# Four sums of weight quarters from VectorE to GpSimd, and two second-level sums one step later, in routed attention with an MLP

## The chip, the cores and the metric

The kernel runs on one core of a Trainium2 chip. The core has five engines, each with its own instruction stream: TensorE (PE, matmuls), VectorE (DVE), ScalarE (ACT), GpSimd (POOL) and SyncE (SP, which here issues the DMAs). Engines wait for each other by semaphores only. VectorE, ScalarE and GpSimd work on SBUF; GpSimd is not used on PSUM, where the matmul results lie. The metric is the device time of one execution in microseconds, and of several executions the median.

## The reference

Two blocks follow each other. The first is attention with a routing mask: 4 batches, 8 heads, 768 positions, 64 dimensions. Each query and each key is assigned to the nearest of 16 centroids, and a query sees only the keys of its own cluster.

```python
q_assign = argmax(einsum(q_n, c_n)); k_assign = argmax(einsum(k_n, c_n))
scores = where(q_assign == k_assign, q @ k.T / 8, -1e9)
attn = exp(scores - max) / (sum + 1e-9);  out = attn @ v
```

The result, as 3072 tokens of 512 numbers, goes through an MLP with weights w_in (512 x 2048) and w_out (2048 x 512), all in float32:

```python
h = x @ w_in
g = h * erf(softplus(h))
return g @ w_out
```

## The kernel before

**Attention.** Two heads are a pair; there are 16 pairs (0 to 15). Each pair is worked in six periods, i = 0 to 5, written out in `period(p, i)`. A period covers two units, a unit being 128 keys against 384 queries of both heads. For each unit PE forms the masked scores (tile sc), ScalarE takes the exponential (pr), GpSimd adds the pr of a half up (`accumulate`, into part of more_out), and PE multiplies by v (into the PSUM bank turned). At the same time the bounds of the next half are found: PE writes products of lowered q and k to the PSUM tile wide, and VectorE reduces them (nmx). There is one wide tile, so PE cannot write the next pass before nmx has been read. At i = 3, `similarities` and `choose` begin the routing of the pair after the next: PE writes a turned bank, VectorE transposes it to sims, and PE needs that bank again for the sums of `divide`, which form at i = 0 and i = 3 from GpSimd's accumulated sums.

**Weights.** During attention w_in and w_out are also loaded and brought to the form in which the MLP uses them: ScalarE (`size`, `rest`, `sign`), VectorE (`bounded`, `shifted`) and GpSimd (`summed`) work on one block after another; in the profile these are the VectorE and GpSimd steps on w_out in pairs 9 to 15.

**Forms.** The MLP's matrix products use seven block products in place of eight, and for that sums and differences of the quadrants of w_in are made ahead, called forms. `left_forms` gives four of them for a pair of column groups f and f + 1: new[0] = a21 + a22, new[1] = new[0] - a11, a21 = a11 - a21, new[2] = a12 - new[1]. The new ones lie in more_in, the third replaces a part of w_in. The column groups f = 0, 2, 4, 6 give four quarters, 16 forms, each a 128 x 512 step. They stand in the list `forms`, in order, each with a version for VectorE and one for GpSimd; four forms of x for chunk 0 are appended behind pair 13. `FORMS` says how many VectorE takes in which period of which pair, and `POOL_FORMS` in which pairs GpSimd takes one at i = 1. What is left at the end, VectorE takes. Before, GpSimd takes 8 of the w_in forms in pairs 8 to 15 and VectorE 8, of which four lie in pairs 12, 13 and 14.

**Behind the attention.** The MLP works in chunks of 512 tokens. `hidden(0, 0)` makes the first half of the hidden columns of chunk 0 (quarters 0 and 1), `hidden(0, 1)` the second half (quarters 2 and 3). Each has four rounds of seven products, and VectorE and ScalarE add the products up from PSUM banks: six that rotate, and two, turned, from the end of attention on. Beside this, the last four blocks of w_out are made ready (`weights`, in `aside_work`), and GpSimd makes second-level forms: `forms_twice` builds 18 sums from w_in and its forms, in the staging tiles a_s and x_own, and each is stored to DRAM (w_dram) by an SP issue. Their order is fixed: four are made at once behind the attention, three ahead of GpSimd's first `summed`, eight behind a fence in `hidden(0, 1)`, and the rest (three) behind that stage. The staging tile x_own is the place of x of chunk 1, so `load_x(1)` waits for the last store. The fences are one-column steps of GpSimd that wait for a step of VectorE.

**Order.** TensorE, VectorE, ScalarE and GpSimd instructions stay in the order in which the program records them, and so do the SP issues of the attention; the SP issues behind it are placed by the scheduler and then run in that order. Line L137 in the profile is the helper through which nearly all of these instructions are recorded, so groups are told apart by tile names.

Of the kernel before, what the change touches and what calls it, by code (L numbers as in the profile page):

```python
# [35 lines left out]
HT, HK, HF, HM = CT // 2, DM // P // 2, NFT // 2, DM // 2  # L36
# [1 line left out]
LC = 512  # L38

UP = 2.0**16  # L40
FORMS = {12: {0: 1}, 13: {0: 1}, 14: {0: 1, 3: 1}, 15: {0: 1, 3: 2, 4: 2, 5: 2}}
POOL_FORMS = range(8, 16)
BIG = 2.0**60
FLOOR = 2.0**50
EPS = 2.0**-70
# [71 lines left out]
BY_VECTOR = 4  # L117
MADE_BEFORE = (3, 0, 0, 0)
MADE = (0, 8)
LAST_AT = (3, 6, 9, 12, 15, 18, 21)  # L120
EARLY_OUTERS = 6
STORE_AFTER = 2
# [23 lines left out]
def kernel(  # L146
# [13 lines left out]
    te, ve, ae, ge = (  # L160
        InOrder(tc, e, in_order) for e in (nc.tensor, nc.vector, nc.scalar, nc.gpsimd)
    )
# [49 lines left out]
    def part_of(i, lo, n):  # L212
        return more_out[:, i].rearrange("p f m -> p (f m)")[:, lo : lo + n]
# [103 lines left out]
    def size_and_rest(n):  # L317
        size(n)
        rest(n)
# [112 lines left out]
    def vectors(p, nm):  # L432
        if p < NPAIR:
            ae.copy(out=pairs[p][nm + "v"], in_=pairs[p][nm + "T"])
# [139 lines left out]
    def divide(u):  # L574

        p, half, _ = units[u]
        st = pairs[p]
        av = st["av", half]

        psum = turned[1 - half][:, 0:QW]  # L580
        for g in range(4):
            te.matmul(psum[g * Q : (g + 1) * Q], lhsT=minus, rhs=st["acc", half][:, g], start=True, stop=True)

        if u + 1 < len(units):
            inv = routep.tile([P, QW], F32, name="inv")
            den = routep.tile([P, QW], F32, name="den")
        else:
            inv, den = part_of(0, 4 * HW, QW), part_of(1, 0, QW)
        ae.activation(out=inv, in_=psum, func=ACT.Ln, bias=alleps, scale=-1.0)
        ae.activation(out=inv, in_=inv, func=ACT.Exp, scale=-1.0)  # L590
        yield
        ve.scalar_tensor_tensor(
            out=den, in0=psum, scalar=S * EPS, in1=inv, op0=ALU.subtract, op1=ALU.mult
        )
        for k in range(2):
            raw = av[:, k, 0:QW]
            ve.scalar_tensor_tensor(
                out=raw, in0=raw, scalar=av[:, k, QW : QW + 1], in1=inv, op0=ALU.add, op1=ALU.mult
            )
        yield  # L600
        x = part_of(0, (2 * p + half) % 4 * HW, HW).rearrange("p (k x) -> p k x", k=2)
        ve.scalar_tensor_tensor(
            out=x, in0=den.unsqueeze(1).to_broadcast([P, 2, QW]), scalar=2.0, in1=av[:, :, 0:QW],
            op0=ALU.add, op1=ALU.mult,
        )
        b, r = divmod(p, HP)
        for g in range(4):
            rows_of, at = r * P + g // 2 * D, b * S + half * HW + g % 2 * QW
            nc.sync.dma_start(
                out=x_dram[rows_of : rows_of + D, at : at + QW].rearrange("(k r) x -> r k x", k=2),  # L610
                in_=x[g * Q : (g + 1) * Q],
            )
        if half == 1:
            del pairs[p]
        yield
# [16 lines left out]
    def left_forms(engine, a11, a12, a21, a22, new):  # L632

        return [
            functools.partial(plus_of, new[0], a21, a22, engine),
            functools.partial(minus_of, new[1], new[0], a11, engine),
            functools.partial(minus_of, a21, a11, a21, engine),
            functools.partial(minus_of, new[2], a12, new[1], engine),
        ]
# [10 lines left out]
    def lefts(a11, a12, a21, a22, new):  # L650
        return {1: a11, 2: a12, 3: new[2], 4: a22, 5: new[0], 6: new[1], 7: a21}
# [7 lines left out]
    def w_in_parts(f, n):  # L659
        c1, c2 = slice(f * P, (f + n) * P), slice((HF + f) * P, (HF + f + n) * P)  # L660
        return (
            w_in[:, 0:HK, c1], w_in[:, HK:, c1], w_in[:, 0:HK, c2], w_in[:, HK:, c2],
            [more_in[:, i, :, c1] for i in range(3)],
        )
# [317 lines left out]
    def last_forms_twice():  # L982
        work = {}
        for o, p in zip(GROUPS[1][1], LAST_AT):
            w = lefts(*w_in_parts(0, HF))[o]
# [339 lines left out]
    def run(work):  # L1325
        for _ in work:
            pass
# [3 lines left out]
    def step_ahead(u, behind=False):  # L1331
        p, i = divmod(u + NJ, 2 * NJ)
        steps = maxima_step(p, i, behind=behind) if p < NPAIR else iter(())
        if not behind:
            run(steps)
        return steps

    forms = []
    for f in range(0, HF, 2):
        forms += zip(*(left_forms(e, *w_in_parts(f, 2)) for e in (ve, ge)))  # L1340
    routing = [iter(())]
    part = [iter(())]
# [1 line left out]
    def period(p, i):  # L1344
        u = 2 * NJ * p + 2 * i
        n1, n2 = 2 * p - 1, 2 * p
        early = lambda n: 0 <= n < N_EARLY

        def mask(place):
            which = (MASKS if p else FIRST_MASKS).get((i, place))  # L1350
            if which:
                return masks(p + 1, *which, turned[0 if i in (0, 5) else 1], place > 1, ve if i == 0 else ae)
            return lambda: None

        if u > 0:
            for which in turns if i in (0, 3) else ():
                turn(*which)
                turns.remove(which)
            step_ahead(u)
        mask(0)()  # L1360
        next(part[0], None)
        if i == 5:
            next(routing[0], None)
        if i == 0 and p:
            run(routing[0])
        if u == 2:
            next(routing[0])
        products(u)
        products(u + 1)
        mask(1)()  # L1370
        second = step_ahead(u + 1, True) if u > 0 else iter(())
        next(second, None)
        rows = D if u == 0 or u + NJ >= len(units) else Q
        scores(u, rows)
        next(second, None)
        if i:
            next(second, None)
        next(part[0], None)
        scores(u + 1, rows)
        later = mask(2)  # L1380
        if i == 0:
            later()
            later = lambda: None
            next(second, None)
        if i == 3:
            similarities(p + 2)
            routing[0] = choose(p + 2, sc_of[u + 1][:, 0], True)
        curve(u)
        later()
        curve(u + 1)  # L1390
        if u == 0:
            step_ahead(1)
            similarities(1)
            routing[0] = choose(1, turned[0])
            next(routing[0])
            next(routing[0])
            vectors(1, "q")
            vectors(1, "k")
        if i == 0 and early(n1 - 1):
            bounded(n1 - 1)  # L1400
            shifted(n1 - 1)
            sign(n1 - 1)
        elif i == 1 and early(n1):
            size_and_rest(n1)
        elif i == 3 and early(n1):
            bounded(n1)
            sign(n1)
        elif i == 5 and early(n2):
            rest(n2)
        for _ in range(min(len(forms), FORMS.get(p, {}).get(i, 0))):  # L1410
            forms.pop(0)[0]()
        if i == 3:
            next(routing[0], None)
            if early(n1):
                shifted(n1)
            for _ in range(2):
                next(routing[0], None)
        elif i == 1:
            load(p + 1, "v", v, vp)
            if p == 0:  # L1420
                run(routing[0])
                transposes(2, "q")
        elif i == 2:
            transposes(p + 2, "k")
        elif i == 4:
            vectors(p + 2, "k")
            vectors(p + 2, "q")
        elif i == 5:
            transposes(p + 3, "q")
        if u > 0:  # L1430
            if i == 1 and p in POOL_FORMS and forms:
                forms.pop(0)[1]()
            if i == 1 and early(n1 - 1):
                summed(n1 - 1)
            elif i == 4 and early(n1):
                summed(n1)
            for w in (u - 2, u - 1):
                accumulate(w)
            for w in (u - 2, u - 1):
                attend(w)  # L1440
            if i % HJ == 0:
                part[0] = divide(u - 1)
                next(part[0])
        if i == 3 and early(n2):
            size(n2)
# [73 lines left out]
    for w in (u - 2, u - 1):  # L1519
        attend(w)  # L1520
    last = divide(u - 1)
    attention.close()

    psb = pool("psb", 6, space=PSUM)
# [22 lines left out]
        GROUPS[1][1][:EARLY_OUTERS],  # L1547
        (actp.tile([P, 2 * FG * HT], F32, name="a_s"), x_of[1].rearrange("p k t -> p (k t)")),
    )
    for _ in range(4):  # L1550
        next(making)()
    queues[0] = store_queue[0] = nc.sync

# [24 lines left out]
    def make():  # L1578
        next(making, idle(1)[0])()

    aside_work += (
        together(idle(2) + gates(0, 0, (0,)), [make] * MADE[0])
        + [lambda: fence(sums_of[0, 0, 0][:, 2, 0, 0:1])] + [make] * MADE[1]
    )
# [65 lines left out]
```

## Time and profile before

| | us |
|---|---|
| median of three runs | 964.12 (963.8 to 964.22) |
| profiled execution, its own time | 963.84 |
| its span | 962.0 |
| granted TensorE clock | 0.999 |
| pairs 12 to 14 | 314 to about 390 |
| first matmul of the MLP | 411.2 |

The span is that of the engines' instructions; the execution's own time is 1.84 us longer. In a line of a timeline the columns are start, duration, engine, source line, operation, output tile, input tiles, shapes and a count, and in brackets how long the engine stood idle before it and what ended that. A group of equal steps is merged into one line. PE is TensorE with matmuls, PEld its weight loads. The chain of waits follows the work that ended last back through what released it.

### The profile page before, as it was taken

What the parts mean: (1) busy time and instruction counts of PE and PEld (TensorE: products, weight loads), DVE (VectorE), ACT (ScalarE), POOL (GpSimd) and SP (SyncE); (2) the same over time, 40 slices, a digit from 0 to 9 for tenths busy, and PEclk for the clock granted to TensorE, in tenths of its full rate; (3) what the DMA queues carried; (4) which work ended last, traced back from release to release, by engine and by line L of the source; (5) the groups of instructions that cost most, each with busy time, mean ns of one, the idle gap of its engine ahead of it and who ended that gap; (6) DMA issues with size and microseconds to landing.
All of it is one profiled execution on the core that took longest, in us unless ns stands there. A gap on an engine that the chain in (4) does not pass through costs nothing.

```text
span 962.0 us, 22444 instructions
## 1 busy us (share of the span) xinstructions
PE 951.3 (99%) x8954; PEld 727.9 (76%) x8954; DVE 800.8 (83%) x1399; ACT 539.0 (56%) x815; POOL 531.4 (55%) x371
## 2 busy tenths in 40 slices
PE   8999999999999999999999999999999999999998
PEld 3555555555555555588888888998999899989987
DVE  8888888888888887787679889788868987897887
ACT  3777777777777777552523541654257236625541
POOL 1688888888888888877579910360054016202600
PEclk9999999999999999999999999999999999999999
DMA  9345445544554521151403444463445436343533
GB/s 222 63 111 112 111 111 111 112 112 110 105 117 83 116 55 52 27 173 41 168 1 154 171 144 136 136 204 110 154 125 172 113 129 209 110 148 120 154 116 110
DMA packets 172313, 116.06 MB, mean 121 GB/s; under 512 B 131376, under 2 KB 141104, under 8 KB 172208
## 3 DMA queue, kind: packets, MB, share of 16 engines
q1 hardware_dynamic: 169280, 113.41, 42.5%
q8 instruction: 71, 1.16, 0.5%
q10 hardware_dynamic: 2928, 1.21, 0.4%
q14 instruction: 34, 0.28, 0.1%
HBM read 90.21 MB, written 24.38 MB: 119 GB/s over the span
## 4 chain that ended last, share of the span: by engine, by line
PE 95%; DVE 3%; DMA 1%; issue 0%; SPq 0%; ACT 0%; DVEq 0%; ACTq 0%
PE bank L137 42%; PE turned L137 31%; PE sc L137 16%; PE wide L137 6%; DVE nmx L137 1%; DMA out_dram<-osb 0%; DVE w_out L137 0%; DMA in_k<-in_k_dram 0%; DVE osb L137 0%; SPq L137 0%; DVE kT L137 0%; DVE km L137 0%; DVE sims L137 0%; DVE more_in L137 0%; DVE qT L137 0%
## 5 line engine op out<-in xcount | busy, mean ns | idle before, releaser
L137 POOL TENSOR_TENSOR more_out<-more_out,pr 128x768 f32<-128x768 f32 x128 | 217.2, 1697 | 16.9 <-ACT pr L137 7.6
L137 DVE TENSOR_REDUCE nmx<-wide 128x2 f32<-128x768 f32 x189 | 180.5, 955 | 46.4 <-PE wide L137 45.9
L137 ACT ACTIVATE pr<-sc 128x768 f32<-128x768 f32 x192 | 148.7, 810 | 89.8 <-PE wide L137 72.8
L137 POOL TENSOR_TENSOR g<-g 128x512 f32<-128x512 f32 x36 | 47.1, 1309 | 217.6 <-DVE g L137 215.7
L137 PE MATMUL turned<-pr,in_v 128*32 128x193 f32 x3072 | 144.8, 330 | 0.0
L137 PEld LDWEIGHTS turned<-pr,in_v 128*32 128x32 f32 x3072 | 91.5, 109 | 50.7 <-issue 21.3
L137 PE MATMUL sc<-qT,kT 64*128 64x384 f32 x528 | 98.4, 486 | 0.0
L137 DVE TENSOR_TENSOR g<-g 128x512 f32<-128x512 f32 x114 | 79.1, 694 | 16.5 <-PE bank L137 12.9
L137 DVE TENSOR_TENSOR g<-a_s,g 128x512 f32<-128x512 f32 x80 | 72.4, 931 | 5.6 <-ACT a_s L137 5.6
L137 DVE TENSOR_TENSOR g<-bank,g 128x256 f32<-128x256 f32 (+1 forms) x129 | 63.9, 522 | 14.8 <-PE bank L137 7.2
L137 PE MATMUL bank<-w_out,g 128*128 128x256 f32 x328 | 75.7, 380 | 0.0
L137 ACT ACTIVATE a_s<-g 128x1024 f32<-128x1024 f32 (+1 forms) x36 | 41.0, 1149 | 55.9 <-POOL g L137 45.3
L137 PE MATMUL bank<-g_more,g 128*128 128x256 f32 x304 | 71.8, 379 | 0.0
L137 PE MATMUL bank<-x_own,w_in 128*128 128x128 f32 (+1 forms) x432 | 71.6, 308 | 0.0
L137 POOL TENSOR_TENSOR more_out<-pr,pr 128x768 f32<-128x768 f32 x32 | 58.9, 1840 | 19.9 <-ACT pr L137 19.9
L137 PEld LDWEIGHTS bank<-w_out,g 128*128 128x128 f32 x328 | 62.0, 190 | 9.6 <-issue 1.4
L137 PEld LDWEIGHTS <-qv 64*128 64x128 bf16 x384 | 27.0, 93 | 55.2 <-issue 39.2
L137 PE MATMUL wide<-kv,qv 64*128 64x384 bf16 x378 | 64.1, 328 | 2.5 <-DVE nmx L137 1.8
L137 PEld LDWEIGHTS sc<-qT,kT 64*128 64x128 f32 x528 | 49.6, 187 | 21.6 <-ACT inv L137 3.1
L137 ACT ACT_TABLE_LOAD x40 | 51.3, 1283 | 22.8 <-DVE g L137 22.2
L137 PEld LDWEIGHTS bank<-x_own,w_in 128*128 128x128 f32 x432 | 61.1, 191 | 4.0 <-issue 0.6
L137 PEld LDWEIGHTS bank<-g_more,g 128*128 128x128 f32 x304 | 57.8, 190 | 7.9
(243 smaller groups left out, 2062.4 us busy)
## 6 DMA issues: line engine op xcount, KB each, us to landing
g_more<-b_dram SPq DMA_DIRECT2D x48, 512.0 KB, 3.6
g_more<-w_dram SPq DMA_DIRECT2D x84, 256.0 KB, 2.8
x_own<-in_moe_w_in_dram SPq DMA_DIRECT2D x13, 512.0 KB, 5.5
in_v<-in_v_dram SPq DMA_DIRECT2D x32, 192.0 KB, 3.2
x_dram<-more_out SPq DMA_DIRECT2D x128, 48.0 KB, 1.7
x_own<-x_dram SPq DMA_DIRECT2D x6, 1024.0 KB, 5.3
in_k<-in_k_dram SPq DMA_DIRECT2D x59, 96.0 KB, 2.6
in_q<-in_q_dram SPq DMA_DIRECT2D x58, 96.0 KB, 4.9
```

What stands on the lines that cost most here:

```text
L137: ins = getattr(self.engine, name)(*args, **kw)
```

## The change

The list `forms` loses the last quarter: it runs over f = 0, 2, 4 and has 12 forms of w_in. `FORMS` loses its entries for pairs 12, 13 and 14 (four forms) and keeps those of pair 15. GpSimd takes one form in each of pairs 8 to 15 at i = 1, as before (`POOL_FORMS` is now a table of periods). The four forms of the last quarter are made by GpSimd behind the last `accumulate` and ahead of the second-level forms. Of the latter, two (`AHEAD`) in place of four are made at once; all 18 keep their order, so each of the later groups begins two forms earlier in it, and the last group has five in place of three.

```diff
-FORMS = {12: {0: 1}, 13: {0: 1}, 14: {0: 1, 3: 1}, 15: {0: 1, 3: 2, 4: 2, 5: 2}}
-POOL_FORMS = range(8, 16)
+FORMS = {15: {0: 1, 3: 2, 4: 2, 5: 2}}
+POOL_FORMS = {p: (1,) for p in range(8, 16)}
...
+AHEAD = 2
...
     forms = []
-    for f in range(0, HF, 2):
+    for f in range(0, HF - 2, 2):
         forms += zip(*(left_forms(e, *w_in_parts(f, 2)) for e in (ve, ge)))
...
-            if i == 1 and p in POOL_FORMS and forms:
+            if i in POOL_FORMS.get(p, ()) and forms:
                 forms.pop(0)[1]()
...
     last = divide(u - 1)
+    for work in left_forms(ge, *w_in_parts(HF - 2, 2)):
+        work()
     attention.close()
...
-    for _ in range(4):
+    for _ in range(AHEAD):
         next(making)()
```

On the engines this comes to four VectorE instructions fewer and four GpSimd instructions more, two GpSimd instructions with their two SP stores in a later place, and, on PE, a wait for GpSimd at the first three products of the third round of `hidden(0, 1)` that read forms of the last quarter. TensorE's, ScalarE's and SyncE's instructions are the same in kind and number.

## The prediction

> **What bounds the kernel now.** I read the page's table of engines and the chain first, then the waits of PE, then the timelines of PE, VectorE (DVE) and GpSimd (POOL) around each of them. The first two lines say that TensorE is the kernel: 951.3 of 962.0 us, 95% of the chain. Time can be won only where PE stands still.
>
> ```profile
> PE 951.3 (99%) x8954; PEld 727.9 (76%) x8954; DVE 800.8 (83%) x1399; ACT 539.0 (56%) x815; POOL 531.4 (55%) x371
> PE 95%; DVE 3%; DMA 1%; issue 0%; SPq 0%; ACT 0%; DVEq 0%; ACTq 0%
> ```
>
> PE has no wait in the profile between 55 and 306 us, and none after 411 us. Between 306 and 384 us, which are pairs 12 to 14, it has five, 2.61 us in all (0.45 + 0.76 + 0.45 + 0.45 + 0.50):
>
> ```profile
> 318.24 0.34 PE L137 MATMUL wide<-kv,qv 64*128 64x384 bf16 x2 [0.45 <-DVE nmx L137]
> 329.70 0.53 PE L137 MATMUL turned<-more_out,minus 128*32 128x192 f32 x8 [0.76 <-DVE sims L137]
> 344.24 0.34 PE L137 MATMUL wide<-kv,qv 64*128 64x384 bf16 x2 [0.45 <-DVE nmx L137]
> 369.28 0.34 PE L137 MATMUL wide<-kv,qv 64*128 64x384 bf16 x2 [0.45 <-DVE nmx L137]
> 379.84 0.53 PE L137 MATMUL turned<-more_out,minus 128*32 128x192 f32 x8 [0.50 <-POOL more_out L137]
> ```
>
> The km instruction runs once a pair, so its starts are a ruler. Pair 11 lasts 24.47 us, pair 12 26.00, pair 13 25.04; pairs 2 to 7 last 24.43 to 24.45 each by the same row.
>
> ```profile
> 289.97 0.62 DVE L137 TENSOR_SCALAR km<-turned,nbig 128x384 bf16<-128x384 f32 x1 [0.55 <-PE turned L137]
> 314.44 0.62 DVE L137 TENSOR_SCALAR km<-turned,nbig 128x384 bf16<-128x384 f32 x1 [0.55 <-PE turned L137]
> 340.44 0.62 DVE L137 TENSOR_SCALAR km<-turned,nbig 128x384 bf16<-128x384 f32 x1 [0.54 <-PE turned L137]
> 365.48 0.62 DVE L137 TENSOR_SCALAR km<-turned,nbig 128x384 bf16<-128x384 f32 x1 [0.54 <-PE turned L137]
> ```
>
> VectorE's timeline shows what stands in front of the waits. In pair 12 the form (more_in, 0.68 us) lies between two w_out steps and the reduction nmx that PE waits for. Later in the pair a w_out step takes 1.39 us where pair 11's took 0.42, and the transpose sims behind it is late.
>
> ```profile
> 302.64 0.42 DVE L137 TENSOR_SCALAR w_out<-w_out 128x512 f32<-128x512 f32 x1
> ...
> 315.84 0.88 DVE L137 TENSOR_SCALAR w_out<-w_out 128x512 f32<-128x512 f32 x2
> 316.63 0.68 DVE L137 TENSOR_TENSOR more_in<-w_in 128x512 f32<-128x512 f32 x1
> 317.23 0.95 DVE L137 TENSOR_REDUCE nmx<-wide 128x2 f32<-128x768 f32 x1
> 327.68 1.39 DVE L137 TENSOR_SCALAR w_out<-w_out 128x512 f32<-128x512 f32 x1
> ```
>
> GpSimd's timeline gives the reason: in pairs 12 and 14 its own form waits 2.6 us for VectorE's, and its sums of pr then end at 328.8 us, over the slow w_out step; in pair 11 they ended at 302.74.
>
> ```profile
> 295.78 6.96 POOL L137 TENSOR_TENSOR more_out<-more_out,pr 128x768 f32<-128x768 f32 x4
> 317.39 1.27 POOL L137 TENSOR_TENSOR more_in<-more_in,w_in 128x512 f32<-128x512 f32 x1 [2.61 <-DVE more_in L137]
> 321.80 6.98 POOL L137 TENSOR_TENSOR more_out<-more_out,pr 128x768 f32<-128x768 f32 x4
> 368.43 1.27 POOL L137 TENSOR_TENSOR more_in<-more_in,w_in 128x512 f32<-128x512 f32 x1 [2.62 <-DVE more_in L137]
> 427.50 1.30 POOL L137 TENSOR_TENSOR w_out<-w_out,g_more 128x512 int32<-128x512 int32 x1 [1.94 <-ACT w_out L137]
> 450.27 0.19 POOL L137 TENSOR_TENSOR u<-g_more 128x1 f32<-128x1 f32 x1 [5.96 <-DVE g_more L137]
> 487.76 0.19 POOL L137 TENSOR_TENSOR u<-g 128x1 f32<-128x1 f32 x1 [17.90 <-DVE g L137]
> ```
>
> **Part 1: VectorE loses four forms in pairs 12 to 14** (one at i = 0 of each, one at i = 3 of pair 14); 4 x 0.68 us. PE, ScalarE and SyncE keep their instructions. GpSimd still makes one form a pair, but its inputs now come from its own earlier forms, so the two waits of 2.6 us for VectorE have nothing left to wait for. In pair 11, which has the same w_out steps and a GpSimd form but no VectorE form, PE never waits; that is my model for the changed pairs.
> - The waits at i = 0 (three of 0.45): nmx ends 3.18 us behind km in pair 11 (292.20 + 0.95 - 289.97), and PE asked for the bank at 3.35 (318.24 - 0.45 - 314.44). Without the form there is 0.17 us to spare. All three go.
> - The 0.76 in pair 12: without its wait GpSimd's sums end 12.8 us behind km, as in pair 11, and the w_out step starts at 12.7 and takes 0.42 again. It goes. Pair 13, where GpSimd's form had no wait, shows no such stall.
> - The 0.50 in pair 14: GpSimd's sum ended at 379.78, and PE wanted it at 379.34, less 0.45 from the wait before, so 13.4 behind km; at 12.8 the sum is 0.6 us early. It goes.
> The price by pair: 26.00 - 24.47 = 1.53 in pair 12, 25.04 - 24.47 = 0.57 in pair 13 (each a little over its waits, since PE starts again slower), and for pair 14, which has no km behind it, its waits alone, 0.95. Sum -3.05. Ends: -2.61 (waits alone) and -3.3 (pair 14 with the same quarter on top).
>
> **Part 2: pair 15.** VectorE's seven forms and GpSimd's one stand where they stood and are of the same kinds, for other columns. Columns of quarters 0 and 1, which the first hidden block needs at 411 us, are now complete at 391 us (pair 15, i = 0). Cost 0.
>
> **Part 3: GpSimd's four forms behind the last sums.** Each is 1.27 us (the more_in<-more_in,w_in row), 5.1 us, starting at 414.57 in the old clock. ScalarE's first copy of a bank waited 4.65 us for GpSimd; it waits for the last sum of pr, which still stands before the forms, so it is not later. PE needs these columns in the third block row of hidden(0,1), 448 us; they are there at 420. Cover: 28 us. Cost 0.
>
> **Part 4: two second-level forms move back** (2 x 1.27 us and two stores on SP). Until the first weight is summed GpSimd has 5.1 - 2.5 = 2.6 us more: that sum ends at 428.1 instead of 425.56, and the next, due at 427.50, 0.7 us late; the 1.94 us of idle time covers the rest, and the fence with 5.96 us of idle stands behind both. On SP the third and fourth a_s stores come about 1.5 us later, and the four x_dram stores of the last unit queue behind them; these are columns of the last batch, read long after. Behind the fence GpSimd has 13 forms instead of 11: the last three stores become five, the load of x for chunk 1 (issued at 467.7, landed by about 473.5 by the DMA shares) comes 2.6 us later, 476.1. VectorE takes it at 475.99 without waiting now, so it waits about 0.1 us, and the four steps on x end at 478.8 against PE's need at about 485 (chunk 1's first block). The w_out forms behind it end at 472.5 instead of 469.85; the next fence idles 17.9 us. Cost on PE 0; if this cover were gone, at most the 2.6.
>
> **The one doubt is VectorE beside a busier GpSimd** between 425.6 and 428.2, when it empties PE's banks. Its w_out steps there take 0.42 us when GpSimd is idle and 0.84 to 1.49 when it works; steps that read a bank keep 0.41. One or two more become slow: 0.4 to 2.1 us. A bank is refilled after six other fills: the one read at 427.29 to 427.71 is filled again at 429.26, the one done at 427.04 at 428.39, so 1.35 to 1.55 us are to spare. I take 0 (one slow step is 0.4 to 1.07), bounds 0 and 0.8 (two at 1.07 less 1.35).
>
> A rule speaks against the change. The Trainium skill, GPSIMD Engine Reference, section 4.1 Engine selection, gives two-input elementwise work to VectorE, with GpSimd about 2x slower. The rows agree on the ratio (1267 against 683 ns). By the rule the four forms lose 4 x 0.58 = 2.3 us of engine time, and counted on the path the sum would be -0.7 us; by the waits above they leave a place where PE stands and go to one where it does not, and the sum stays -3.05.
>
> **The sum** against the profiled execution's own 963.84 us: 963.84 - 3.05 = 960.8. The median of the runs, 964.12, lies 0.28 above that execution; I say 960.9. A measurement of this kernel can tell about 0.2%, 1.9 us, from no change, so the forecast is faster by more than that (0.32%), with 1.1 us in hand.
>
> **Rivals.**
> - Half of it stays (13%): GpSimd's sums stay late in pairs 12 and 14 for another reason (its w_out sum also waits for ScalarE, 1.1 to 2.4 us in most pairs), so 0.76 + 0.32 of pair 12 and 0.50 stay: 1.58. For it: the slow w_out step meets GpSimd by only 0.1 us in pair 11. Against it: pairs 8 to 11 never stall. Time 963.84 - 1.47 = 962.4.
> - Part is given back in the first hidden stage (8%): two to three slow w_out steps more than the banks cover, 1 to 2 us of PE. Time 961.9 to 962.8.
> - Slower (6%): the same place, but each of the eight w_out steps between 419 and 433 us (1.39, 0.84, 1.49, 0.42, 1.14, 0.42, 0.42, 0.42, together 6.54) takes 1.49: 11.92, so 5.4 us, and the banks cover nothing. It decides from 3.05 us on, and past 5.0 us shows as slower. Time 963.84 - 3.05 + 5.4 = 966.2. Against it: half of these steps run where GpSimd's load is unchanged.
> - The change does nothing (2%): PE waits at the same places for other VectorE work. Time 964.
>
> **Numbers.** Forecast 71%, all faster. The first rival straddles: 3 of its 13 to faster. Second: 3 of 8 to faster. Faster 0.77, same 0.17, slower 0.06. Range: from 963.8 - 3.3 less 0.3 of scatter, 960.2, up to the second rival's 962.8, which takes in the first.
>
> **What would show it.** Right: PE has no wait between 306 and 384 us; km steps of 24.4 to 24.6 us in pairs 12 and 13; GpSimd's forms in pairs 12 and 14 without a wait; the w_out step near 12.7 us behind km at 0.42; four GpSimd forms before the first a_s; PE still without waits from the end of attention on. Wrong: a PE wait on g or on a bank within 25 us of the first bank matmul, a PE wait for x near 74 us behind it, or a sims wait that stays in pair 12.

## The result

| | before | after |
|---|---|---|
| median of seven runs, us | 964.01 (963.73 to 964.22) | 960.8 (960.48 to 961.08) |
| profiled execution, its own time | 963.84 | 960.8 |
| its span | 962.0 | 959.1 |

The ratio is 0.9966, with a 95% interval of 0.9954 to 0.9978: 3.2 us less, where 960.9 us was forecast. On a second chip the same kernel gave 0.9975 (0.9964 to 0.9986), 961.64 against 963.83 us, with single runs from 960.67 to 962.24. A few tenths of a microsecond between two medians therefore say little, and the experiments below are read in their traces: of each stage by its length, and within a stage by the starts of PE's matmuls, which are the same 8954 in the same order in all these kernels and can be compared one by one.

The page of the changed kernel, table of engines and chain: PE has the same work, VectorE four instructions and 3.0 us less, GpSimd four instructions and 6.9 us more, and the span is 2.9 us shorter.

```profile
PE 951.2 (99%) x8954; PEld 727.5 (76%) x8954; DVE 797.8 (83%) x1395; ACT 538.7 (56%) x815; POOL 538.3 (56%) x375
PE 96%; DVE 2%; ACT 1%; issue 0%; DMA 0%; DVEq 0%; SPq 0%; ACTq 0%
```

The trace marks no wait of PE any more behind the first 55 us. It leaves out idle time under 0.15 us and counts it from the end of the matmul ahead; delays that it does not mark are told below. VectorE's timeline has the ruler again (km, once a pair), and behind it in pair 12 the w_out step and the transpose sims:

```profile
314.80 0.62 DVE L138 TENSOR_SCALAR km<-turned,nbig 128x384 bf16<-128x384 f32 x1 [0.55 <-PE turned L138]
339.41 0.62 DVE L138 TENSOR_SCALAR km<-turned,nbig 128x384 bf16<-128x384 f32 x1 [0.55 <-PE turned L138]
363.85 0.62 DVE L138 TENSOR_SCALAR km<-turned,nbig 128x384 bf16<-128x384 f32 x1 [0.55 <-PE turned L138]
...
327.48 0.42 DVE L138 TENSOR_SCALAR w_out<-w_out 128x512 f32<-128x512 f32 x1
327.94 0.58 DVE L138 STREAM_TRANSPOSE sims<-turned 128x384 f32<-128x384 f32 x1
```

GpSimd's timeline of pair 12: the form starts at once, without the wait of 2.61 us, and the four sums end at 327.58, 12.78 us behind km.

```profile
315.08 1.29 POOL L138 TENSOR_TENSOR more_in<-w_in 128x512 f32<-128x512 f32 x1
317.45 1.28 POOL L138 TENSOR_TENSOR w_out<-w_out,x_own 128x512 int32<-128x512 int32 x1 [1.09 <-ACT x_own L138]
320.61 6.97 POOL L138 TENSOR_TENSOR more_out<-more_out,pr 128x768 f32<-128x768 f32 x4
```

Pair 14 has no km behind it, but PE's own sums at i = 0 (turned from more_out and minus) give its length. PE's timeline of the changed kernel:

```profile
364.97 0.51 PE L138 MATMUL turned<-more_out,minus 128*32 128x192 f32 x8
388.73 0.51 PE L138 MATMUL turned<-more_out,minus 128*32 128x192 f32 x8
```

Before, these two started at 366.60 and 391.64. So the kernel by stages, in us:

| stage | before | after | difference |
|---|---|---|---|
| start to km of pair 12 | 314.44 | 314.80 | +0.36 |
| pair 12, km to km | 26.00 | 24.61 | -1.39 |
| pair 13, km to km | 25.04 | 24.44 | -0.60 |
| pair 14, sums at i = 0 to the next | 25.04 | 23.76 | -1.28 |
| pair 15, to the MLP's first matmul | 19.59 | 19.58 | 0 |
| MLP, to the end of the span | 550.77 | 550.79 | 0 |

The gain is 3.27 us, all of it in pairs 12 to 14. The 0.36 at the start were there before any changed instruction (the first km starts at 11.69 us in place of 11.30). Between the km of pair 14 and its sums lie 1.12 us in both kernels, which no row counts. The 0 of the MLP is a sum of two: matmul by matmul, PE falls 0.34 us back at 473 us, which the section on the forms behind the attention explains, and gains 0.38 us at 695 us, at a matmul that before had waited 0.12 us for ScalarE's osb. No changed instruction stands there, and the cause of this gain is open.

### The profile page after: what moved, and what is told of

The parts are those of the page before. It is cut to its first block, busy times and chain, and to the rows that moved or that the text cites. A ratio compares the mean times of both kernels' runs of the same rounds, so it can differ in the third digit from the quotient of the medians.

```text
span 959.1 us, 22447 instructions
## 1 busy us (share of the span) xinstructions
PE 951.2 (99%) x8954; PEld 727.5 (76%) x8954; DVE 797.8 (83%) x1395; ACT 538.7 (56%) x815; POOL 538.3 (56%) x375
## 4 chain that ended last, share of the span: by engine, by line
PE 96%; DVE 2%; ACT 1%; issue 0%; DMA 0%; DVEq 0%; SPq 0%; ACTq 0%
PE bank L138 42%; PE turned L138 32%; PE sc L138 17%; PE wide L138 6%; DVE nmx L138 1%; ACT a_s L138 0%; ACT L138 0%; DVE g L138 0%; DMA in_q<-in_q_dram 0%; DVE kT L138 0%; DVE osb L138 0%; DVE g_more L138 0%; DVE sims L138 0%; DVE qT L138 0%; DVE turned L138 0%
```

## The experiments

What is undecided behind such a table is the cause: the work taken from VectorE, its place in front of nmx, or GpSimd's wait for it; and whether what was put behind the attention is really free. Each kernel below is the changed one with one edit. Both kernels with VectorE's forms, GpSimd busy and four forms ahead ran on a chip on which the changed kernel itself was not run; their medians are read against the kernel before, and their stages against the changed kernel's trace. The traces are compared by the same stages:

| kernel | pair 12 | pair 13 | pair 14 | MLP | median | ratio to before |
|---|---|---|---|---|---|---|
| before | 26.00 | 25.04 | 25.04 | 550.77 | 964.01 | 1 |
| changed | 24.61 | 24.44 | 23.76 | 550.79 | 960.8 | 0.9966 |
| changed, second chip (again) | 24.63 | 24.44 | 23.74 | 550.84 | 961.64 | 0.9975 |
| VectorE's forms, own chain, i = 0 | 25.08 | 25.07 | 24.36 | 550.97 | 962.35 | 0.9984 |
| the same at i = 1 | 24.78 | 24.75 | 24.08 | 550.46 | 961.34 | 0.9976 |
| GpSimd waits (pool_waits) | 25.96 | 24.44 | 25.00 | 550.82 | 963.69 | 0.9999 |
| GpSimd busy (pool_late) | 26.16 | 24.43 | 25.21 | 550.75 | 963.85 | 1.0002 |
| four forms ahead | 24.60 | 24.45 | 23.75 | 551.66 | 961.63 | 0.9978 |
| eight forms ahead | 24.62 | 24.44 | 23.77 | 556.79 | 966.62 | 1.0028 |
| last quarter left out | 24.61 | 24.48 | 23.72 | 550.59 | 961.87 | 0.9980 |

The intervals of the ratios are 0.0008 to 0.0012 to either side.

### The four forms on VectorE again, without a chain to GpSimd

```diff
+OWN = {12: (0,), 13: (0,), 14: (0, 3)}
...
+    own = left_forms(ve, *w_in_parts(HF - 2, 2))
...
+        for _ in range(OWN.get(p, ()).count(i)):
+            own.pop(0)()
...
-    for work in left_forms(ge, *w_in_parts(HF - 2, 2)):
-        work()
```

> As the changed kernel, but the last quarter's four forms are made by VectorE again, at i = 0 of pairs 12, 13 and 14 and at i = 3 of pair 14, as before the change; they are now a chain of their own, so GpSimd's form in pairs 12 and 14 waits for none of them, and GpSimd makes no forms behind the attention. Theory (three waits of PE come straight from the VectorE form in front of the nmx reduction; the waits in pairs 12 at sims and 14 at GpSimd's sum come from GpSimd's form waiting for VectorE's): each of the three pairs is 0.5 to 0.6 us longer than in the changed kernel, no wait at sims and none on GpSimd's sum: 960.8 + 1.6 = 962.4 us. Rival A (the sheer VectorE work in pairs 12 to 14 is what costs): all of the gain is gone, 964.0. Rival B (only GpSimd's lateness costs): 960.8.

Measured: 962.35 us, ratio 0.9984 (0.9975 to 0.9993). PE's timeline has the three waits at i = 0 back, of 0.5 us each, and no other in these pairs:

```profile
318.87 0.34 PE L139 MATMUL wide<-kv,qv 64*128 64x384 bf16 x2 [0.50 <-DVE nmx L139]
343.93 0.34 PE L139 MATMUL wide<-kv,qv 64*128 64x384 bf16 x2 [0.48 <-DVE nmx L139]
...
369.01 0.34 PE L139 MATMUL wide<-kv,qv 64*128 64x384 bf16 x2 [0.49 <-DVE nmx L139]
```

The pairs are 0.47, 0.63 and 0.60 longer, 1.70 in all. Both rivals fall: the VectorE work costs about half of the gain, not all of it and not nothing. The fourth form, at i = 3 of pair 14, shows no price: pair 14 is no dearer than pair 13.

### The same work in another place

```diff
-OWN = {12: (0,), 13: (0,), 14: (0, 3)}
+OWN = {12: (1,), 13: (1,), 14: (1, 4)}
```

> The same four VectorE forms as a chain of their own, but at i = 1 of pairs 12, 13 and 14 and at i = 4 of pair 14, where VectorE idles 0.96 us for PE before an nmx; nothing else differs from the kernel with the forms at i = 0. Theory: the place costs and not the work, so the idle time takes the 0.68 us and PE has no new wait: 960.8, at most 961.2. Rival A (the work itself): 962.4 to 964.0.

Measured: 961.34 us, ratio 0.9976 (0.9966 to 0.9985). No wait of PE is marked in these pairs, as expected, and yet they are 0.17, 0.31 and 0.32 longer than in the changed kernel, 0.80 in all. VectorE's timeline of pair 12 shows the form ahead of an nmx that is pushed back by it (in the changed kernel it began at 320.72, behind 0.28 us of idle time), and the later w_out step at 0.68 in place of 0.42:

```profile
320.35 0.74 DVE L139 TENSOR_TENSOR more_in<-w_in 128x512 f32<-128x512 f32 x1
321.01 0.95 DVE L139 TENSOR_REDUCE nmx<-wide 128x2 f32<-128x768 f32 x1
...
327.54 0.68 DVE L139 TENSOR_SCALAR w_out<-w_out 128x512 f32<-128x512 f32 x1
```

So the place decides more than half of the form's price, but I was wrong that idle time of VectorE takes it for nothing: the 0.96 us in front of nmx begins only behind this reduction. The rest reaches PE by the same two paths, in delays too short to be marked as waits. Matmul by matmul, PE falls behind the changed kernel by 0.05, 0.11 and 0.07 us at one write of wide in each pair (322.01, 346.78, 371.53) and by 0.24 at another in pair 14 (383.57); each of these starts some 0.04 us behind the end of the nmx that it needs. At the sums behind the late sims in pairs 12 and 13 (328.85, 353.60) it falls back by 0.11 and 0.21 us. These six make 0.79 of the 0.80 us.

### GpSimd late, VectorE untouched: first by work

```diff
+            if i == 1 and p in (12, 14):
+                for _ in range(2):
+                    left_forms(ge, *w_in_parts(HF - 2, 2))[0]()
```

> The changed kernel, VectorE without forms in pairs 12 to 14, but GpSimd makes one form twice more ahead of its own form in pairs 12 and 14 (2 x 1.27 us, about the 2.6 us that it waited before the change; the step is repeated, the values stay). Theory: GpSimd's sums end some 1.5 us later in these two pairs, the w_out step of VectorE meets them and takes 1.4 in place of 0.42 us, PE waits about 0.76 at sims in pair 12 and about 0.5 for GpSimd's sum in pair 14, and the pairs are 0.8 and 0.7 us longer: 960.8 + 1.5 = 962.3. Rival A (VectorE's work): 960.8, no wait. Rival C (these two waits came from VectorE being 0.45 us late and not from GpSimd): 960.8.

Measured: 963.85 us, ratio 1.0002 (0.9994 to 1.0011). More than the theory's 962.3, and the traces say why: the two extra GpSimd steps ran beside VectorE's w_out steps at i = 0, which took 1.87 in place of 0.92 us for the two, and made a wait on nmx of their own. PE's timeline:

```profile
318.99 0.34 PE L138 MATMUL wide<-kv,qv 64*128 64x384 bf16 x2 [0.84 <-DVE nmx L138]
330.22 0.53 PE L138 MATMUL turned<-more_out,minus 128*32 128x192 f32 x8 [0.52 <-DVE sims L138]
...
369.59 0.34 PE L138 MATMUL wide<-kv,qv 64*128 64x384 bf16 x2 [0.85 <-DVE nmx L138]
379.93 0.53 PE L138 MATMUL turned<-more_out,minus 128*32 128x192 f32 x8 [0.28 <-POOL more_out L138]
```

The waits at sims and at GpSimd's sum are there without any VectorE form, but the edit brought a second cause in, so it does not separate them.

### GpSimd late by a wait alone

```diff
+            if i == 1 and p in (12, 14):
+                late = w_steps[n1 - 1][0][:, 0:1].bitcast(I32)
+                for _ in range(4):
+                    ge.tensor_tensor(out=small.tile([P, 1], I32, name="late"), in0=late, in1=late, op=ALU.add)
```

> The changed kernel, VectorE without forms in pairs 12 to 14, but GpSimd's form in pairs 12 and 14 waits again: four one-column steps (some 0.7 us together), of which the first reads what VectorE's two w_out steps at i = 0 write, stand in front of it, so it starts about 2.9 us behind km as before the change, and GpSimd does nothing beside those two VectorE steps. Theory (the sims wait and the wait on GpSimd's sum come from GpSimd's wait alone): no wait of PE on nmx, about 0.76 us at sims in pair 12 and 0.5 to 0.9 on GpSimd's sum in pair 14, pairs 12 and 14 longer by about 0.8 and 0.7 us: 1.5 us above the changed kernel. Rival C (they came from VectorE's lateness at i = 0): as the changed kernel, no wait.

Measured: 963.69 us, ratio 0.9999 (0.9991 to 1.0008); on the same chip the changed kernel had 961.64. GpSimd idles 2.03 us and its sums end 14.3 us behind km; VectorE's two w_out steps at i = 0 keep their 0.88, and the one at i = 3 takes 1.94. GpSimd's and VectorE's timelines of pair 12:

```profile
317.13 0.62 POOL L138 TENSOR_TENSOR late<-w_out 128x1 int32<-128x1 int32 x4 [2.03 <-DVE w_out L138]
322.10 6.97 POOL L138 TENSOR_TENSOR more_out<-more_out,pr 128x768 f32<-128x768 f32 x4
```

```profile
316.18 0.88 DVE L138 TENSOR_SCALAR w_out<-w_out 128x512 f32<-128x512 f32 x2
327.42 1.94 DVE L138 TENSOR_SCALAR w_out<-w_out 128x512 f32<-128x512 f32 x1
329.28 0.57 DVE L138 STREAM_TRANSPOSE sims<-turned 128x384 f32<-128x384 f32 x1
```

PE's timeline has just the two waits that the theory named, and no wait on nmx:

```profile
329.99 0.53 PE L138 MATMUL turned<-more_out,minus 128*32 128x192 f32 x8 [1.31 <-DVE sims L138]
...
379.52 0.53 PE L138 MATMUL turned<-more_out,minus 128*32 128x192 f32 x8 [1.08 <-POOL more_out L138]
```

The mechanism is shown, and its size is not what I expected: alone, GpSimd's wait makes pairs 12 and 14 1.33 and 1.26 us longer (25.96 and 25.00 less the 24.63 and 23.74 of that chip), nearly all that they lost before the change, and not the 0.8 and 0.7 that were left for it after the form's own 0.45 to 0.6. The two causes do not add. With the form, PE comes about half a microsecond later to the place where it then waits for sims, so that much of GpSimd's lateness is already paid: in the kernel before PE falls back by 0.56 us at wide and then by 0.82 at sims, here by 1.38 at sims alone. Form alone 0.47, wait alone 1.33, both together 1.39 in pair 12; 0.60, 1.26 and 1.28 in pair 14.

The slow steps fit a rule. The Trainium skill, SBUF — State Buffer, section Who interferes with whom, says that GpSimd and some VectorE instructions share a pair of ports as an exclusive lock, so the one that comes second is blocked until the first has ended. Here a step of 0.42 us took 1.94: it came at 327.42, just behind the start of the last sum of 1.7 us, and its end, 329.36, lies 0.29 us behind the end of that sum, 329.07. The kernel before (329.07 behind 328.78) and the one with GpSimd busy (329.58 behind 329.29) show the same 0.29. The step is blocked to the end of the sum that ran when it came, as the rule has it.

### Are the forms behind the attention free?

```diff
-    for work in left_forms(ge, *w_in_parts(HF - 2, 2)):
-        work()
...
+            if i == 4 and 3 <= p < 6:
+                ge.memset(more_in[:, p - 3, :, (HF - 2) * P :], 0.0)
```

> The changed kernel with the last quarter's four forms left out (their three tiles are filled with zeros by GpSimd in pairs 3 to 5, and the fourth, a part of w_in, stays as loaded), so the products that use them are of other numbers. Theory: the 5.1 us of GpSimd behind the attention are wholly covered, so this is as the changed kernel, within 0.2 us. Rival E (they cost something, by VectorE steps that meet them): up to 1 us below the changed kernel.

Measured: 961.87 us, ratio 0.9980 (0.9971 to 0.9988), against 0.9975 of the changed kernel on that chip. The medians do not compare, since the zero fills made the time up to pair 12 1.45 us longer (km at 316.20 in place of 314.75). The MLP took 550.59 us against 550.84, so the four forms cost about 0.25 us.

The place can be read. In chunk 0's product with w_out, PE needs VectorE's sum g_more, which stands behind VectorE's gate products. GpSimd's w_out forms have moved back and run beside these products, three of which take 3.69 us in place of 1.88. Timelines of VectorE and of the weight loads (PEld), before and then in the changed kernel:

```profile
470.67 1.88 DVE L137 TENSOR_TENSOR g<-a_s,g 128x512 f32<-128x512 f32 x3
475.66 0.84 PEld L137 LDWEIGHTS bank<-more_out,g_more 128*128 128x128 f32 x4
```

```profile
467.45 3.69 DVE L138 TENSOR_TENSOR g<-a_s,g 128x512 f32<-128x512 f32 x3
468.28 1.72 POOL L138 TENSOR_TENSOR more_out<-more_out,w_out 128x512 f32<-128x512 f32 x1
473.19 0.94 PEld L138 LDWEIGHTS bank<-more_out,g_more 128*128 128x128 f32 x5 [0.47 <-DVE g_more L138]
```

PE falls 0.34 us behind the kernel before at this product, and 0.32 to 0.36 in the three other traces that have both moves. Without the four forms behind the attention it is 0.08 here, and 0.07 and 0.08 in the two kernels that make them on VectorE. The chain between can be followed: with the four forms GpSimd is late with its w_out forms in the second hidden stage, VectorE's first gate product there takes 1.14 in place of 0.69 us beside them, GpSimd's fence opens 38.64 in place of 38.19 us behind the MLP's first matmul, and all that GpSimd does behind the fence is later by about as much. So all but a quarter of a microsecond of the 5.1 us is covered, and what is not goes the way of rival E.

### The two forms that were moved back

```diff
-AHEAD = 2
+AHEAD = 4
```

> The changed kernel with four second-level forms made at once behind the attention, as before, in place of two: GpSimd is 2.5 us later with the first two sums of the late w_out blocks, and VectorE empties the banks beside a GpSimd that never idles. Theory: the banks have 1.3 us to spare and the fence idles 6 us, so nothing reaches PE: 960.8. Rival D (the move of the two forms is what keeps the first hidden stage free of waits): one or two more slow steps of VectorE beyond the banks' slack, 961.5 to 963.

Measured: 961.63 us, ratio 0.9978 (0.9969 to 0.9987). The median alone would not decide, since the changed kernel gave 960.8 and 961.64; the trace does. The MLP is 0.87 us longer, and PE has two waits that the changed kernel does not have, though not in the first hidden stage, where both the theory and its rival had looked, but in the second:

```profile
447.47 1.10 PE L138 MATMUL bank<-x_more,more_in 128*128 128x256 f32 x4 [0.32 <-DVE g L138]
449.01 1.10 PE L138 MATMUL turned<-x_own,w_in 128*128 128x256 f32 x4 [0.43 <-DVE g L138]
```

In front of them VectorE makes the products of the gate, g<-a_s,g, between its bank steps. The timelines of VectorE and GpSimd with four forms ahead, and then of the changed kernel:

```profile
440.75 3.05 DVE L138 TENSOR_TENSOR g<-a_s,g 128x512 f32<-128x512 f32 x2 [1.76 <-ACT a_s L138]
...
441.54 1.71 POOL L138 TENSOR_TENSOR more_out<-more_out,w_out 128x512 f32<-128x512 f32 x1
```

```profile
440.40 1.74 DVE L138 TENSOR_TENSOR g<-a_s,g 128x512 f32<-128x512 f32 x2 [1.34 <-ACT a_s L138]
...
439.72 1.26 POOL L138 TENSOR_TENSOR more_out<-more_out,w_out 128x512 f32<-128x512 f32 x1
```

With two ahead GpSimd's w_out forms end at 440.98, 0.6 us behind the start of the products; with four they end at 443.25, two products take 3.05 in place of 1.74 us, and the banks behind them are emptied late. PE falls back by 1.2 us at the two waits. In return it does not lose the 0.34 us at g_more, where with four ahead GpSimd's later work is done in time. So the move back is worth 0.87 us on the whole: without it the four forms behind the attention would have cost about 1.2 us. Three forms ahead, between the two, were not run.

### More of the same

```diff
-AHEAD = 2
+AHEAD = 8
```

> The changed kernel with eight second-level forms made at once in place of two, so GpSimd is 7.6 us later with the late w_out sums and the w_out forms behind them. Theory, from the kernel with four: GpSimd's w_out forms then run beside the four products g<-a_s,g and the four g_more sums of VectorE in the second hidden stage, each of these eight takes up to 1.4 in place of 0.68 us, the banks are emptied late, and PE waits there 3 to 5 us in all, none in the first hidden stage: 2.5 to 5 us above the changed kernel. Rival F (the 0.8 us at four forms come from the first hidden stage's slow w_out steps): waits of PE before 440 us, and in the second stage no more than at four.

Measured: 966.62 us, ratio 1.0028 (1.0017 to 1.0039), 5.0 us above the changed kernel of that chip: the theory's range, at its end (5.8 us between the two profiled spans). PE's waits are again all in the second hidden stage, 3.91 us, so the first stage's w_out steps (the rival) are out:

```profile
447.33 1.13 PE L138 MATMUL bank<-x_own,w_in 128*128 128x256 f32 x4 [1.17 <-DVE g L138]
450.77 1.10 PE L138 MATMUL bank<-x_more,more_in 128*128 128x256 f32 x4 [2.31 <-DVE g L138]
452.30 2.04 PE L138 MATMUL turned<-x_own,w_in 128*128 128x256 f32 x4 [0.43 <-DVE g L138]
```

The MLP is 6.0 us longer, 2.1 more than the waits. Most of the missing part begins in the last of these lines, where four matmuls take 2.04 us in place of 1.03, and is nothing that the theory had; it is told at the end.

## Why the prediction was right

**The waits at i = 0, three of 0.45: right.** They are gone, and the kernel with VectorE's forms, without a wait of GpSimd for them, brings back just these.

**The 0.76 and the 0.50: right in cause.** GpSimd's form no longer waits, and with a wait put back PE waits at the same two instructions.

**The prices by pair: the sum near, two terms off.** I took -1.53, -0.57 and -0.95, in all -3.05; measured were -1.39, -0.60 and -1.28, in all -3.27. In pair 12 I set the length of pair 11 as the end; 0.14 us stayed. The w_out step ends 13.09 us behind km as in pair 11 of the same trace, but sims starts at 13.14 in place of 13.00, and PE's sums behind it come 0.11 us late; why sims starts later is open. In pair 14 I counted the marked waits alone, 0.95. PE's lateness there is more, 0.56 and 0.69 us at the two places, and the upper bound that I kept, a quarter more, holds 1.2 of the 1.28. My reason for the excess, that PE starts again slower, was wrong: the lateness is whole at the waiting matmul itself. In the changed kernel that matmul of pair 12 starts at 318.04, 0.11 us before the one ahead of it ends, and the mark of a wait, 0.45 where PE lost 0.56, leaves this overlap out.

**One wrong picture under a right sum.** I split pair 12 by its waits, 0.45 for the form and 0.76 and a rest for GpSimd, and priced the first rival with what that left, 1.58 in two pairs. The wait alone costs 2.59 in these pairs. Late arrivals at one place give the later of them and not the sum; had the forms gone and GpSimd's wait stayed, the gain would have been about 0.7 us and not the rival's 1.47.

**Pair 15: right**, at 0. **The forms behind the attention: 0.25 us and not 0.** The cover that I counted, 28 us up to the product that reads these forms, held. The cost came from what GpSimd does behind them, by way of VectorE's g_more.

**The second-level forms: a cost near 0 was right, the reason was not.** I looked for cover in GpSimd's own idle time, and the fence idles 5.96 us as before. That idle time is cover for whoever waits for GpSimd. It is none for VectorE, whose gate products run in it and take up to 1.75 in place of 0.68 us beside GpSimd's forms (four ahead). My bound for a lost cover of 2.6 us, "at most the 2.6", was not reached: the two forms put ahead again cost 0.87 us, and six more cost 6.0 for 7.6 us of GpSimd. The doubt that I named, VectorE beside a busier GpSimd, was the right one at the wrong place: the eight w_out steps of the first hidden stage took 6.04 us in all, less than the 6.54 before, and PE's losses came 20 us later with four and eight forms ahead, and 46 us later, 0.34 us, in the change itself.

**The load of x for chunk 1.** VectorE did not wait for it. It came to it 1.5 us later by the stage's own clock, since the gate products ahead of it were slow, the same that made g_more late.

**The total.** That 960.9 was said and 960.8 measured is closer than the reasoning earned. The pairs gave 0.22 us more than the sum, 0.36 were lost ahead of them and 0.34 at g_more, which the sum put at nothing, and 0.38 were gained at 695 us for a cause that is open. On the second chip the gain of the medians was 2.2 us.

**The rivals.** Of the first, at most the 0.14 us in pair 12 were seen. The second and the third name the kind of mechanism that the kernels with four and eight forms ahead then had, a VectorE slowed beside GpSimd so that banks are emptied late, though in other steps and in a later stage; in the change itself the same slowing cost the 0.34 us at g_more.

## What to carry to other kernels

An instruction on a second engine can cost twice: in front of what PE waits for, and through a third engine that waits for its result. Look for both, undo each alone, and do not add their prices where they meet at one place. Idle time of GpSimd ahead of a fence is not free for more GpSimd work if VectorE uses it for steps that slow down beside GpSimd, as here the gate products with their two SBUF inputs and the w_out steps: before work is moved there, look at what VectorE does in just that stretch. And where a trace marks no wait and a stage is yet longer, compare the matmuls' starts one by one.

## What the hardware showed

The kernel with eight forms ahead lost 2.1 us more than PE's marked waits. Its stretches of time, with the busy time and number of instructions of PE, PEld, DVE, ACT and POOL, the granted TensorE clock, the DMA share and GB/s:

```profile
449.00:451.00 2.00, 0.23 (x1) 0.26 (x2) 2.00 (x3) 0.00 (x0) 0.74 (x1) 1.00 0.00 0
451.00:453.00 2.00, 1.57 (x6) 1.05 (x6) 1.79 (x5) 0.00 (x0) 1.10 (x2) 0.81 0.00 0
453.00:455.00 2.00, 2.00 (x7) 1.55 (x6) 1.90 (x6) 0.00 (x0) 1.92 (x3) 0.50 0.33 131
455.00:457.00 2.00, 2.00 (x9) 1.75 (x8) 1.69 (x6) 0.00 (x0) 1.92 (x2) 0.83 0.46 180
```

PE was busy for some 1.5 of 5 us between 446 and 451, with 2.31 us as the longest wait, and the granted clock then went to 0.50 and was back at 1.0 by 457. Matmul by matmul against the changed kernel, PE lost 1.74 us from 452.30 to 455.76, while the clock was low; the rest is 0.67 us at the three waits beyond their marks, less the 0.34 us at g_more, which this kernel does not lose. With four forms ahead the waits of 0.32 and 0.43 us left the clock at 1.0. The Trainium skill, TensorE: Matmul & The Clock Gate, Part 1, describes a gate that sets the clock to half or full by how busy PE has lately been; the 0.50 here agrees with its half. So here two waits of 0.75 us in all cost PE 1.2 us and no clock, and 3.5 idle microseconds out of 5 cost the clock as well; where between the two the clock gives way, these runs do not show.
